# Loading the last 96 rows of a weight matrix as 68 + 28 rows, in two transfers with a semaphore each

## The chip, the cores and the metric

The kernel runs on one core of a Trainium2 chip. The metric is the device time of one execution in microseconds (us). A ratio compares the fast runs of two kernels of the same rounds and stands here, with its 95% interval, as the record has it; it is not quite the ratio of the medians or means that are quoted. Where "means" are given, it is the difference between the mean of a kernel's runs and that of the runs of before beside it.

Of the engines, PE multiplies matrices (PEld is the weight load that comes before each product), DVE computes on vectors, and SP issues the loads here.

## The reference, cut to what matters

One token of two sequences goes through a decode step: layer norm, attention of 32 heads over 8192 cached positions, a residual, layer norm, a gated feed-forward block (D = 512, F = 1376), a residual.

```python
h  = x + attention(layernorm(x), k_cache, v_cache, wq, wo)   # caches: 2 x 32 x 8192 x 128, bf16
g  = layernorm(h) @ W_gate                                   # 512 x 1376
u  = layernorm(h) @ W_up
h2 = h + (max(g, 0) * u) @ W_down                            # 1376 x 512
```

The caches are 256 MiB and are read once. W_down has 1376 rows: ten blocks of 128 and a rest of 96. The change is about that rest.

## The kernel before

K and V of a pair of heads come as one transfer each, into four slots. At the end slot 0 is free and takes W_up, W_gate and the first 1280 rows of W_down; the last 96 rows have a buffer of their own, `wd_last`, with one row in each partition. SP issues all of these in a row, 25 to 28 us before they are first used:

```python
WD_BLOCKS = ((0, 4), (4, 4), (8, 2))
# ... (cut)
wd_last = sb("wd_last", [FR, D], BF16)                       # FR = 96, D = 512: 1 KB a row
# ... (cut) SP, when slot 0 is free:
for k, w in enumerate((B_W_up, B_W_gate)):
    nc.sync.dma_start(slot[0][...], w...).then_inc(sem_w[k], 16)
for k, (r0, n) in enumerate(WD_BLOCKS):
    nc.sync.dma_start(slot[0][...], B_W_down[r0 * 128:(r0 + n) * 128]...).then_inc(sem_wd[k], 16)
nc.sync.dma_start(wd_last[:], B_W_down[F - FR:]).then_inc(sem_wd[3], 16)
```

At the very end PE runs the down projection in the order in which the blocks arrive, with a wait in front of each, then DVE scales and adds the residual, and the result is stored:

```python
order = [(f, k) for k, (r0, n) in enumerate(WD_BLOCKS) for f in range(r0, r0 + n)] + [(10, 3)]
for n, (f, k) in enumerate(order):
    pe.wait((sem_wd[k], 16))
    kp = 128 if f < 10 else FR
    for m in range(4):
        i = nc.tensor.matmul(Op[0][32 * m:32 * m + B, 0:128], lhsT=hd[0:kp, f * B:(f + 1) * B],
                             rhs=(wdn[:, f, :] if f < 10 else wd_last[:])[:, 128 * m:128 * m + 128],
                             start=(n == 0), stop=(n == FC - 1))
```

I call the three WD_BLOCKS transfers block 1, 2 and 3.

The softmax here doesn't subtract the row's maximum and nothing guards it: scores larger than these inputs give would overflow.

## Time and profile before

| | before |
|---|---|
| median, first 3 runs | 660.2 us (660.03 to 660.39) |
| span of the profiled run | 659.2 us |
| HBM traffic | 281 MB at a mean 427 GB/s |
| SP issues the load of wd_last | 628.22 us |
| its 16 landings | 654.13 to 656.06 us |
| PE's first weight load that reads wd_last | 656.28 us |

The page's DMA lines, before. The first row is the busy share of the 16 DMA engines in 40 slices of the span, in tenths:

```profile
DMA  8999999999999999999999999999999999999997
GB/s 366 444 437 431 420 445 416 443 428 431 438 422 441 422 439 433 428 435 424 441 422 439 433 428 433 426 441 422 439 434 426 435 424 441 424 437 433 428 417 295
DMA packets 10653, 281.17 MB, mean 427 GB/s; under 512 B 1202, under 2 KB 1300, under 8 KB 1812
```

The stream never pauses until the last slice. Dividing 281 MB by 427 GB/s gives 658 us, so nearly the whole span is the stream. Only what happens while it runs out can be changed by this edit. The table of windows, before (columns: window, its length, busy time and instruction count of PE, PEld, DVE, ACT and POOL, then granted PE clock, DMA share, GB/s):

```profile
641.00:648.00 7.00, 6.99 (x71) 2.30 (x68) 1.63 (x4) 1.55 (x8) 0.00 (x0) 0.58 0.99 413
...
652.00:653.00 1.00, 1.00 (x35) 0.98 (x36) 0.04 (x1) 0.00 (x0) 0.00 (x0) 0.50 1.02 397
...
654.00:655.00 1.00, 1.00 (x35) 0.98 (x33) 0.00 (x0) 0.00 (x0) 0.00 (x0) 0.50 0.43 157
...
655.50:656.00 0.50, 0.50 (x28) 0.50 (x24) 0.07 (x1) 0.00 (x0) 0.00 (x0) 0.50 0.16 33
656.00:656.50 0.50, 0.50 (x28) 0.41 (x16) 0.00 (x0) 0.00 (x0) 0.00 (x0) 0.50 0.00 0
```

The DMA share falls from 1.02 to 0.16 over three microseconds: the 16 engines run dry one after another. The chain that ended last, in order of time, before (start, duration, what):

```profile
655.13 0.19 DVE hd L789
...
655.36 1.37 PE O L808 x23
...
656.85 0.35 DVE kT L815
```

The end is a chain of compute: the gated product hd, the down projection, the residual. The timeline, before: the issues of W_up and of wd_last on SP, and the weight loads of the down projection.

```profile
625.95 0.33 SPq L699 DMA_DIRECT2D slot<-in_B_W_up_dram  x1
...
628.22 2.39 SPq L706 DMA_DIRECT2D wd_last<-in_B_W_down_dram  x1
...
655.36 0.95 PEld L808 LDWEIGHTS O<-slot,hd 128*2 128x2 bf16 x40 [0.32 <-DVE hd L789]
...
656.28 0.13 PEld L808 LDWEIGHTS O<-wd_last,hd 96*2 96x2 bf16 x4
```

There is no gap in front of the wd_last weight loads: the data came 0.22 us before the first of them. The trace also records each increment that a DMA makes on its semaphore; I call them landings. Here are the latest of them, before, in us (not a view of the profile, but read from the trace):

```
block 3: 16 landings, 653.90 ... 655.57 655.69 655.71 655.86
wd_last: 16 landings, 654.13 ... 655.84 655.91 655.92 656.06
```

### The profile page before, as it was taken

What the parts mean: (1) busy time and instruction counts of PE and PEld (TensorE: products, weight loads), DVE (VectorE), ACT (ScalarE), POOL (GpSimd) and SP (SyncE); (2) the same over time, 40 slices, a digit from 0 to 9 for tenths busy, and PEclk for the clock granted to TensorE, in tenths of its full rate; (3) what the DMA queues carried; (4) which work ended last, traced back from release to release, by engine and by line L of the source; (5) the groups of instructions that cost most, each with busy time, mean ns of one, the idle gap of its engine ahead of it and who ended that gap; (6) DMA issues with size and microseconds to landing.
All of it is one profiled execution on the core that took longest, in us unless ns stands there. A gap on an engine that the chain in (4) does not pass through costs nothing.

```text
span 659.2 us, 7582 instructions
## 1 busy us (share of the span) xinstructions
PE 324.3 (49%) x3073; PEld 188.6 (29%) x3073; DVE 469.2 (71%) x280; ACT 213.6 (32%) x431; POOL 73.5 (11%) x125
## 2 busy tenths in 40 slices
PE   2753454435455343655535364443556444354577
PEld 0331332213233121433313142221324222133344
DVE  1585576788767678776768877676886767787991
ACT  1622333143342223334223343422324332333250
POOL 3002002020200202020020201002020110202000
PEclk9856556565756657555665756756555765655656
DMA  8999999999999999999999999999999999999997
GB/s 366 444 437 431 420 445 416 443 428 431 438 422 441 422 439 433 428 435 424 441 422 439 433 428 433 426 441 422 439 434 426 435 424 441 424 437 433 428 417 295
DMA packets 10653, 281.17 MB, mean 427 GB/s; under 512 B 1202, under 2 KB 1300, under 8 KB 1812
## 3 DMA queue, kind: packets, MB, share of 16 engines
q1 hardware_dynamic: 10632, 281.06, 99.3%
q8 instruction: 5, 0.08, 0.1%
q14 instruction: 4, 0.03, 0.0%
q10 hardware_dynamic: 12, 0.00, 0.0%
HBM read 281.05 MB, written 0.00 MB: 426 GB/s over the span
## 4 chain that ended last, share of the span: by engine, by line
DMA 76%; DVE 19%; PE 4%; issue 1%; ACT 1%; SPq 0%; DVEq 0%
DMA slot<-in_A_k_cache_dram 76%; DVE prod L540 16%; DVE prod L549 2%; PE O L405 1%; PE O L463 1%; PE T L381 0%; ACT kT L566 0%; PE W L469 0%; DVE scores L554 0%; PE S L756 0%; PE O L756 0%; PE O L808 0%; PE Ob L417 0%; SPq L172 0%; PE S L364 0%
## 5 line engine op out<-in xcount | busy, mean ns | idle before, releaser
L540 DVE TENSOR_TENSOR prod<-slot,q_c 128x12288 bf16<-128x12288 bf16 x32 | 209.9, 6558 | 148.0 <-DMA slot<-in_A_k_cache_dram 141.3
L405 PE MATMUL O<-slot,e 128*16 128x512 bf16 x1024 | 119.3, 621 | 219.9 <-ACT e L495 146.2
L549 DVE TENSOR_TENSOR prod<-prod 128x6144 bf16<-128x6144 bf16 (+3 forms) x128 | 212.2, 1657 | 7.8
L566 ACT ACTIVATE kT<-T 128x1024 bf16<-128x1024 bf16 x128 | 126.1, 1022 | 144.6 <-PE T L381 141.9
L381 PE MATMUL T<-ident_f,slot 128*128 128x128 f32 x512 | 108.6, 365 | 29.1 <-DVEq L587 29.1
L405 PEld LDWEIGHTS O<-slot,e 128*16 128x16 bf16 x1024 | 26.4, 114 | 287.0 <-ACT e L495 172.9
L495 ACT ACTIVATE e<-scores 64x96 bf16<-64x96 f32 x64 | 19.5, 304 | 239.6 <-DVEq L601 238.9
L381 PEld LDWEIGHTS T<-ident_f,slot 128*128 128x128 f32 x512 | 79.0, 188 | 44.2 <-DVEq L587 43.3
L537 POOL COPY q_c<-q_all 128x136 bf16<-128x136 bf16 x32 | 57.2, 1788 | 195.5 <-DVEq L591 152.5
L364 PE MATMUL S<-q_c,kT 128*128 128x4 bf16 x1024 | 47.4, 168 | 40.8 <-ACT kT L566 40.0
L364 PEld LDWEIGHTS S<-q_c,kT 128*128 128x128 bf16 x1024 | 39.1, 104 | 67.9 <-ACT kT L566 66.8
L417 PE MATMUL Ob<-sel,os_sb 128*128 128x4 f32 x136 | 30.1, 345 | 24.2 <-ACT os_sb L569 24.2
L417 PEld LDWEIGHTS Ob<-sel,os_sb 128*128 128x128 f32 x136 | 28.6, 311 | 26.1 <-ACT os_sb L569 26.1
L520 POOL MEMSET O_l<- 128x40 bf16 (+1 forms) x13 | 1.8, 136 | 303.9 <-DVEq L598 303.9
L554 DVE TENSOR_REDUCE scores<-prod 128x96 f32<-128x768 bf16 x32 | 30.5, 953 | 2.8
L566 ACT ACT_TABLE_LOAD x15 | 19.2, 1283 | 0.3
L495 ACT ACTIVATE e<-S 64x32 bf16<-64x32 f32 x64 | 13.0, 202 | 15.1 <-PE S L364 14.7
L569 ACT ACTIVATE os_sb<-O 128x512 f32<-128x512 f32 x17 | 10.1, 597 | 12.8 <-PE O L405 12.4
L495 ACT ACTIVATION_READ_ACCUMULATOR e<-S 64x1 f32 x64 | 12.8, 201 | 0.7
L495 ACT ACTIVATION_READ_ACCUMULATOR e<-scores 64x1 f32 x64 | 11.8, 185 | 0.0
L426 PEld LDWEIGHTS Ob<-zs,ones_f 128*128 128x128 f32 x30 | 7.1, 296 | 12.5 <-issue 12.5
L525 POOL COPY rsel<-rows 128x30 bf16<-128x30 bf16 x28 | 5.9, 209 | 33.3 <-DVEq L598 32.5
(104 smaller groups left out, 90.6 us busy)
## 6 DMA issues: line engine op xcount, KB each, us to landing
slot<-in_A_k_cache_dram SPq DMA_DIRECT2D x32, 4096.0 KB, 32.1
slot<-in_A_v_cache_dram SPq DMA_DIRECT2D x31, 4096.0 KB, 30.3
slot<-in_A_wq_dram SPq DMA_DIRECT2D x1, 4096.0 KB, 12.2
X<-in_A_wo_dram SPq DMA_DIRECT2D x1, 3840.0 KB, 45.8
slot<-in_A_v_cache_dram SPq DMA_DIRECT2D x1, 3072.0 KB, 23.3
slot<-in_B_W_up_dram SPq DMA_DIRECT2D x1, 1376.0 KB, 23.2
slot<-in_B_W_gate_dram SPq DMA_DIRECT2D x1, 1376.0 KB, 26.2
slot<-in_A_v_cache_dram SPq DMA_DIRECT2D x1, 1024.0 KB, 25.4
```

The lines of the kernel that those rows point to most:

```text
L364: i = nc.tensor.matmul(Sp[p % 2][:, 2 * jj:2 * jj + 4], lhsT=kv_[:, k, r, :], rhs=q_c[p % 2][:, 4 * r:4 * r + 4], start=(r == 0), stop=(r ...
L381: i = nc.tensor.transpose(Tp[g % 2][:, k * 128:(k + 1) * 128], k_t[:, j:j + 2, :].rearrange("p j d -> p (j d)").bitcast(F32), ident_f[:])
L405: i = nc.tensor.matmul(Op[0][c:c + 16, :], lhsT=e_t[q][:, j // VJ, :], rhs=v_t[:, j:j + VJ, :].rearrange("p j d -> p (j d)"), start=(q == ...
L417: i = nc.tensor.matmul(Ob[:, 0:4], lhsT=os_sb[:, jj * Dh:(jj + 1) * Dh], rhs=sel[:, 4 * jj:4 * jj + 4], start=(jj == 0), stop=(jj == VJ - 1))
L426: return nc.tensor.matmul(bank[:, ZC:ZC + 8], lhsT=ones_f[:], rhs=zs[:], start=True, stop=True)
L495: i = nc.scalar.activation(out=e_t[q][h, j0 // VJ:j1 // VJ, 8 * q:8 * q + 8].rearrange("p g (j a) -> p g j a", a=2)[:, :, :, a], in_=src(h ...
L537: nc.gpsimd.tensor_copy(out=q_c[p % 2][:], in_=q_all[:, p]).then_inc(g2d, 1)
L540: return nc.vector.tensor_tensor(out=prod[:, 0:JC, :], in0=tile((2 * p) % 4)[:, 0:JC, :], in1=q_c[p % 2][:, 8:QW].unsqueeze(1).broadcast_t ...
L549: run(nc.vector.tensor_tensor(out=prod[:, 0:JC, 0:w], in0=prod[:, 0:JC, 0:w], in1=prod[:, 0:JC, w:2 * w], op=ALU.add))
L554: return nc.vector.tensor_reduce(out=scores[p % PG][:, 0:JC], in_=prod[:, 0:JC, 0:8], axis=AX.X, op=ALU.add)
L566: to_pe(nc.scalar.activation(out=kT[gg % 2][:], in_=Tp[gg % 2][:].bitcast(BF16), func=ACT.Copy))
L569: to_pe(nc.scalar.activation(out=os_sb[:], in_=Op[0][:], func=ACT.Copy))
```

## The change

The intent is to bring the rest in as two pieces, each with its own semaphore. PE waits for both before the one matmul that reads them, so nothing starts earlier by design.

```diff
+    WD_TAIL = ((0, 68), (68, 28))
...
-        sem_wd = [S(f"wd{i}") for i in range(4)]
+        sem_wd = [S(f"wd{i}") for i in range(5)]
...
-                        nc.sync.dma_start(wd_last[:], B_W_down[F - FR:]).then_inc(sem_wd[3], 16)
+                        for k, (r0, n) in enumerate(WD_TAIL):
+                            nc.sync.dma_start(
+                                wd_last[r0:r0 + n], B_W_down[F - FR + r0:F - FR + r0 + n]).then_inc(sem_wd[3 + k], 16)
...
-                    pe.wait((sem_wd[k], 16))
+                    pe.wait((sem_wd[k], 16), (sem_wd[max(k, 2 * k - 2)], 16))
```

## The prediction

> **What bounds the kernel now.** The stream from HBM. The page shows the 16 DMA engines at 9 tenths in nearly every slice, and 281 MB at a mean 427 GB/s: 658 of the 659.2 us span; the chain that ended last is 76% DMA of the K cache. Only the end is not covered: the table of windows has the DMA share falling from 1.02 (652 to 653 us) to 0.43 (654 to 655), 0.16 (655.5 to 656) and 0. From 641 us the chain, in order of time, is compute: last P·V, normalisation, up, gate, the down projection (1.37 us from 655.36), one DVE instruction (0.35 us), and the store, to 659.2.
>
> **How close wd_last is to that chain.** SP issues it at 628.22 us and it lands 27.8 us later, queued behind other loads. The landing records of its semaphore show 16 increments, one for each DMA engine, from 654.13 to 656.06 us. PE reaches the first weight load of wd_last at 656.28 us without a gap. So the slack is 0.22 us; whatever makes the last engine later by more is on the critical path.
>
> **What the change does.** Same bytes, same 1 KB packets. The Trainium skill, "DMA: Bandwidth & Descriptors", section "Why a DMA increments its semaphore by 16 and not by 1", says that a transfer uses the largest number of engines, up to 16, that divides its slowest dimension. The trace agrees where it can: 96 rows gave 16 landings, each 4-row store 4 completion packets. So 68 rows should go over 4 engines (17 packets each) and 28 rows over 14 (2 each). Four engines carry 19 packets instead of 6, ten carry 2, two none. A 1 KB packet takes 46 ns in the trace, so the four finish about 13 x 46 = 0.6 us later (estimate), the others about 0.2 us earlier.
>
> Whether it costs depends on where those four stand in the 1.9 us spread, which the trace doesn't tell. If one is among the five latest (655.67 to 656.06), the 68 rows land at 656.3 to 656.7, and PE waits 0 to 0.4 us before wd_last. If all are early, nothing happens. I put 65% on some wait.
>
> Other costs: a second issue on SP (96 rows took 2.39 us to issue, 128 rows 0.33 to 0.43), done by about 633 us, when SP has nothing else until 657.2. A second semaphore wait on PE, some tens of ns, on the chain. Nothing that helps is removed: the matmul waits for both parts.
>
> **Predicted.** 660.2 + about 0.2 = 660.4 us, range 659.5 to 661.3 (the runs of before alone spread 0.36 us). Faster by over 2%: 0.5%; within 2%: 99%; slower by over 2%: 0.5%.
>
> **What would show it.** Two wd_last issues, the first with 4 data landings, the second with 14; as many 1 KB packets as before; the 68-row part landing last, 0.3 to 0.7 us later than 656.06 relative to the stream's end; a new gap of PE before wd_last, released by DMA, of up to 0.4 us, and the store later by as much. All before 650 us unchanged. If the four engines are early: both landings before 656.1 and no gap.
>
> **What would make it wrong.** The 68 rows going to one engine only: 68 x 46 ns = 3.1 us, so up to 3 us later. Or a 17-row share far slower than 46 ns a packet. Or the slow SP issue blocking something I don't see. None reaches 2%.

## The result, and the profile after

The median of 6 runs is 660.33 us (660.24 to 660.74), beside 660.17 us (660.03 to 660.39, 6 runs) before. The ratio is 1.0003, with a 95% interval of 0.999 to 1.0016: the same. All outputs are right.

The page, after: the packets. Two more than before, both of the small completion kind.

```profile
DMA packets 10655, 281.17 MB, mean 427 GB/s; under 512 B 1204, under 2 KB 1302, under 8 KB 1814
```

Before, this load had 16 completion packets; 4 + 14 = 18 is two more. The landings in the trace, after:

```
block 3:  16 landings,                      653.86 ... 655.71 655.93 656.09
68 rows:   1 record at 629.81, then  4:     655.00 655.42 655.47 655.86
28 rows:   1 record at 641.06, then 14:     654.10 ... 655.88 656.05 656.14
```

So the 68 rows went over 4 engines and the 28 rows over 14, and the one early record of each comes 0.12 and 0.18 us after SP's issue ended. This agrees with the Trainium skill, "DMA: Bandwidth & Descriptors", section "Why a DMA increments its semaphore by 16 and not by 1", which says that the engines used are the largest divisor up to 16 of the slowest dimension, and that the issuing sequencer adds the missing count at once. But the four engines with 17 packets did not end last. The timeline, after:

```profile
625.45 0.33 SPq L700 DMA_DIRECT2D slot<-in_B_W_up_dram  x1
...
627.74 13.14 SPq L708 DMA_DIRECT2D wd_last<-in_B_W_down_dram  x2
...
654.98 0.31 PEld L811 LDWEIGHTS O<-slot,hd 128*2 128x2 bf16 x16 [0.32 <-DVE hd L792]
...
655.54 0.31 PEld L811 LDWEIGHTS O<-slot,hd 128*2 128x2 bf16 x16 [0.26 <-DMA slot<-in_B_W_down_dram]
656.13 0.10 PEld L811 LDWEIGHTS O<-slot,hd 128*2 128x2 bf16 x8 [0.28 <-DMA slot<-in_B_W_down_dram]
656.24 0.12 PEld L811 LDWEIGHTS O<-wd_last,hd 96*2 96x2 bf16 x4
```

Two things are new. SP spends 13.14 us on the two issues; one line of the tile view of wd_last, after, splits them (minimum/median/maximum, ns):

```profile
L708 SPq DMA_DIRECT2D wd_last<-in_B_W_down_dram x2: 1944/6548/11152, 627.7 to 629.7; - x2
```

And PE now waits for DMA, but in front of blocks 2 and 3, whose loads the change doesn't touch, and not in front of wd_last. The chain that ended last, after, goes through a DMA that is not wd_last either.

```profile
625.82 27.04 DMA slot<-in_B_W_gate_dram
...
652.91 1.73 PE O L759 x44
...
654.75 0.19 DVE hd L792
...
654.98 1.68 PE O L811 x35
...
656.76 0.35 DVE kT L818
```

Compute was ahead of the stream in this profile (the down projection starts at 654.98, against 655.36), and behind it in the profile before. The table of windows, after, shows what went with that: PE was granted a clock of 0.81 in the window of the last P·V products (attention weights times V), against 0.58 before.

```profile
641.00:648.00 7.00, 5.69 (x69) 2.25 (x70) 1.94 (x5) 2.16 (x9) 0.00 (x0) 0.81 1.00 419
```

Nothing in the change touches that stage. The two profiles also differ before it: SP came to the first load for slot 0, that of W_up, at 625.95 us before and at 625.45 us after, and to wd_last only after that, so this much of the difference was there before an edited instruction ran. Over all profiles the issue of W_up lies between 625.18 and 627.92 us. Two single profiles therefore can't say what the change costs, and the experiments begin by repeating both kernels.

### The profile page after: what moved, and what is told of

The parts are those of the page before. It is cut to its first block, busy times and chain, and to the rows that moved or that the text cites. A ratio compares the mean times of both kernels' runs of the same rounds, so it can differ in the third digit from the quotient of the medians.

```text
span 659.0 us, 7584 instructions
## 1 busy us (share of the span) xinstructions
PE 322.5 (49%) x3073; PEld 187.6 (28%) x3073; DVE 469.3 (71%) x280; ACT 213.7 (32%) x431; POOL 73.6 (11%) x125
## 4 chain that ended last, share of the span: by engine, by line
DMA 80%; DVE 18%; issue 1%; PE 1%; SPq 0%; DVEq 0%
DMA slot<-in_A_k_cache_dram 76%; DVE prod L541 16%; DMA slot<-in_B_W_gate_dram 4%; DVE prod L550 2%; PE O L759 0%; PE O L811 0%; DVE scores L555 0%; SPq L173 0%; DVEq L588 0%; DVEq L592 0%; SPq L176 0%; SPq L177 0%; DVE kT L818 0%; DVE hd L792 0%; DVEq L604 0%
## 5 line engine op out<-in xcount | busy, mean ns | idle before, releaser
L406 PE MATMUL O<-slot,e 128*16 128x512 bf16 x1024 | 117.6, 613 | 220.4 <-ACT e L496 146.5
```

Source lines behind the costliest of these rows:

```text
L406: i = nc.tensor.matmul(Op[0][c:c + 16, :], lhsT=e_t[q][:, j // VJ, :], rhs=v_t[:, j:j + VJ, :].rearrange("p j d -> p (j d)"), start=(q == ...
```

## The experiments

Twelve runs of kernels followed, in three groups of four; x1 to x9 and y1 to y5 are their numbers in the table below. The kernels of one group share their 9 runs of before on the same chip. The groups ran on different chips, with medians of before of 660.54, 660.36 and 660.49 us, so an expectation that gives a time is to be read against these. Theory A is that the share of the busiest engine decides, together with where that engine stands in the order in which the engines run dry. The rivals are that the split itself costs something (a second transfer, a second wait), and that wd_last doesn't matter to the time at all.

### Both kernels again

No edit.

> The kernel before, unchanged, to see how far one profile differs from the next. All theories: 660.2 us within 0.2. The landings of wd_last end within about 0.4 us of 656.06 us; PE waits at most 0.2 us in front of wd_last. If the latest landing moves by 0.3 us or more from profile to profile, the 0.16 us between the medians of before and after can't be assigned from two profiles.

> The changed kernel, unchanged. Theory A (share of the engines): 68 rows go over engines that stand early or in the middle of the spread, so their 17 packets are absorbed: the 68-row part lands before the 28-row part, no PE gap before wd_last, time 660.2 to 660.5 us. Rival B (the split itself costs: second wait on PE, second transfer): 0.1 to 0.2 us over the kernel before in every round. The issue of the 28 rows takes about 11 us on SP again.

Measured: before 660.54 us (5 runs) beside 660.54; after 660.71 us beside 660.54, ratio 1.0001. The means differ by -0.07 and by +0.05 us. The second issue on SP took 11.28 us again. The landings of after repeat: the 68 rows end at 655.84, block 3 at 656.16, the 28 rows at 656.33. PE's first wd_last weight load came at 656.43, 0.105 us after the 28 rows; from the step of the loads in front of it (0.107 us for four) it would have come at 656.30, so PE did wait about 0.13 us (estimate), for the 28 rows, where I had expected no gap.

The records of the trace also show what the second wait costs (not a view of the profile; x2, the changed kernel, in us):

```
block 3: last landing 656.155; first weight load, which carries the wait itself, 656.197
28 rows: last landing 656.329; wait instruction (EVENT_SEMAPHORE) 656.358, 0.051 long;
         first weight load of wd_last, which carries the wait for the 68 rows, 656.434
```

A load that carries its only wait starts 0.042 us after the landing; with the extra wait instruction in front of it, 0.105 us. In the kernel before, the load of wd_last carries its only wait and there is no such instruction. So where PE stands at this wait, the second semaphore adds about 0.06 us to the chain.

### The same split with the packets spread as before: 64 + 32

```diff
-    WD_TAIL = ((0, 68), (68, 28))
+    WD_TAIL = ((0, 64), (64, 32))
```

> Two transfers and two waits as in the change, but 64 and 32 rows, which both spread over 16 engines (4 + 2 packets each, as many as before). Theory A: as before, 660.2 us within 0.15, 16 landings each, last landing about 0.25 us after the last of the third W_down block. Rival B: as the change, 660.3 to 660.4. SP issues of 0.33 to 0.45 us each if only counts that are no power of two are slow to issue, else 2 us and more.

Measured: 660.66 us beside 660.54, ratio 1.0000; means +0.08 us. Each part has 16 landings. The last comes 0.33 us after the last of block 3, against 0.20 us of x1: a second transfer on the same engines lands later, even with the same packets in all (0.33 us again in y3, and 0.20 to 0.25 us in the three profiles of before). The SP issues took 0.61 and 1.15 us, which neither branch of my guess about powers of two foresaw. The split costs nothing that this can resolve.

### One engine takes nearly everything: 89 + 7

```diff
-    WD_TAIL = ((0, 68), (68, 28))
+    WD_TAIL = ((0, 89), (89, 7))
```

> Two transfers, but 89 rows, a prime, so that one engine should carry 89 packets, and 7 rows over seven engines. Theory A (the share of the busiest engine decides, at 43 to 46 ns a packet): that engine lands 3.9 to 4.1 us after its part of the third block (654.2 to 655.1 us), so at 658.1 to 659.2; PE waits 1.8 to 3.0 us before wd_last; 662.2 to 663.3 us. Rival C (wd_last is not near the critical path, or the split costs the same at every size): 660.3 us.

Measured: 662.18 us beside 660.54, ratio 1.0025 (1.0011 to 1.0038), means +1.64 us. The 89 rows have a single data landing, at 657.77; the last of the 7-row part comes at 657.95. The timeline of 89 + 7:

```profile
655.66 0.94 PEld L811 LDWEIGHTS O<-slot,hd 128*2 128x2 bf16 x40 [0.32 <-DVE hd L792]
...
658.06 0.12 PEld L811 LDWEIGHTS O<-wd_last,hd 96*2 96x2 bf16 x4 [1.45 <-DMA wd_last<-in_B_W_down_dram]
```

The new wait of 1.45 us in front of wd_last is most of the 1.64 us by which the kernel got slower. Rival C falls: wd_last can hold up the end. The time, the landing and the wait are all under the ranges that I gave, probably because the one engine was among the first to run dry: 89 packets of 43 ns, the spacing of back-to-back packets in the trace, before 657.77 is 653.9, where block 3 had its first landings (653.93). The SP issue of the 7 rows took 21.01 us.

### The parts in the other order: 28 + 68

```diff
-    WD_TAIL = ((0, 68), (68, 28))
+    WD_TAIL = ((0, 28), (28, 68))
```

> The same two parts in the other order: 28 rows first, 68 rows second; the rows of a part differ, not its size. Theory A on the time: the engines' shares are the same, so as the change, 660.3 to 660.7 us beside 660.5 of before; the 68-row part again lands before 656.1 us. On the SP issue, theory Q (the issue of a transfer waits until the one before it fits into the queues of its engines): 28 rows issue in under 2.5 us, and so do the 68 rows, as nothing stands behind them; SP is done by about 633 us. Rival I (28 rows over 14 engines are slow to issue by themselves): 11 us for the 28 rows, now the first.

Measured: 660.3 us beside 660.36, ratio 0.9999. The landings are those of the change (68 rows end at 656.04, 28 rows at 656.13). The timeline of 28 + 68, SP:

```profile
630.01 1.30 SPq L708 DMA_DIRECT2D wd_last<-in_B_W_down_dram  x2
```

The two issues took 0.46 and 0.79 us. So 28 rows are not slow to issue by themselves, rival I falls, and theory Q stands: it is what lies in front that holds up an issue. The runs make a series of it. The issue of the second part took, by the packets that the first part put on each of its engines: 0.79 us after 2 packets (28 + 68), 1.15 us after 4 (64 + 32), 6.39 us after 7 (91 + 5), 11.15 us after 17 (the change), 17.99 us after 43 (86 + 10) and 21.01 us after 89 (89 + 7). The issue of the first part (or of the whole wd_last) varies too: 1.9 to 2.9 us in the six profiles in which SP came to it at 627.5 to 628.2 us, and 0.33 to 0.87 us in the seven in which it came at 629.9 to 630.3 us. That full queues are the reason is inferred from this and from the early load below; no record of the profile shows a queue's fill, and the second parts differ in rows and engines as well.

### 91 + 5

```diff
-    WD_TAIL = ((0, 68), (68, 28))
+    WD_TAIL = ((0, 91), (91, 5))
```

> 91 rows over seven engines (13 packets each) and 5 rows over five (1 each): the engines that landed last in the third block get nothing. Theory A: both parts have landed by 655.9 us, before the third block's last landing (about 656.05); PE never waits for wd_last itself; 660.2 to 660.6 us beside 660.5 of before, so at most 0.2 us gained, since the kernel before has next to no wait there to win back. Rival (the slow engines' 6 packets cost the kernel before something): 0.2 to 0.3 us less in every round.

My expectation was wrong about the engines: 13 also divides 91 and is the larger, and the trace has 13 data landings, not 7. Each had 7 packets. Measured: 660.45 us beside 660.36, ratio 1.0001. Both parts had landed by 655.93, before the last landing of block 3 at 656.17, as expected; and nothing was gained (means +0.15 us). In this profile PE came to wd_last at 656.85 without a wait.

### A middle dose: 86 + 10

```diff
-    WD_TAIL = ((0, 68), (68, 28))
+    WD_TAIL = ((0, 86), (86, 10))
```

> A middle dose: 86 rows over two engines (43 packets each), 10 rows over ten (1 each), so 44 packets on the busiest engine against 6, 19 and 90. Theory A: 44 x 44 ns = 1.9 us after those engines' part of the third block (653.95 to 655.1 us), so they land at 655.9 to 657.0; PE waits 0 to 0.6 us; 660.4 to 661.1 us. A straight line through 6 and 90 packets would give +0.75 us, 661.3; a threshold gives 0.1 to 0.5.

Measured: 660.94 us beside 660.36, ratio 1.0009 (0.9996 to 1.0023), means +0.52 us. The two engines landed at 656.10 and 656.31, the 10-row part at 656.49. The timeline of 86 + 10:

```profile
656.59 0.12 PEld L811 LDWEIGHTS O<-wd_last,hd 96*2 96x2 bf16 x4 [0.23 <-DMA wd_last<-in_B_W_down_dram]
```

This lies just above the branch with a threshold (0.1 to 0.5) and below the straight line (0.75), so it doesn't tell the two apart; the profile, with a wait of 0.23 us, was taken of the fastest of the five runs. Three of the five runs are slower than every run of before in the group, which points to a cost of 44 packets on the busiest engine that 19 don't have; but the interval of the ratio contains 1, so the cost isn't shown clear of noise.

### The parts at the start

```diff
+                for k, (r0, n) in enumerate(WD_TAIL):
+                    nc.sync.dma_start(
+                        wd_last[r0:r0 + n], B_W_down[F - FR + r0:F - FR + r0 + n]).then_inc(sem_wd[3 + k], 16)
                 load(0, A_k_cache, 0)
...
-                        for k, (r0, n) in enumerate(WD_TAIL):
-                            nc.sync.dma_start(
... (cut)
```

> 68 and 28 rows as in the change, but loaded at the start, behind wq and the last rows of wo, into the same buffer, which nothing else uses. Theory A: the end of the stream is then the third W_down block; PE has no wait for wd_last; the total bytes are the same, so the stream ends about as late as before less nothing: 660.2 to 660.7 us. Theory Q on the issue: no backlog stands in front, so both issues take under 1 us; rival I: 28 rows take about 11 us here too.

Measured: 660.63 us beside 660.36, ratio 1.0006 (0.9993 to 1.002), means +0.35 us: no gain, and perhaps a loss (the interval contains 1). In the one profile block 3 landed last, at 656.33, against 655.86 to 656.06 in the three profiles of before. The bytes that now come earlier in the stream could account for 0.23 us of that (an estimate: 96 KiB at 427 GB/s); the rest is not explained. On the issue, theory Q holds again. The timeline of the early load, SP:

```profile
1.72 0.91 SPq L180 DMA_DIRECT2D wd_last<-in_B_W_down_dram  x2
```

With only the loads of wq and of the last rows of wo in front, 68 and 28 rows issue in 0.91 us together, against 13.14 us at the end. The 28 rows stand behind the same 17 packets on each of four engines here and took 0.49 us, so the part in front alone doesn't hold up an issue; it points to all that is still queued.

### Is there a cost of 0.1 to 0.2 us after all?

The first comparison had +0.22 us between the means, the second +0.05. So four kernels ran again, with no new edit.

> The kernel before once more, as the control of this group: within 0.1 us of the runs of before in the same rounds. It gives a third profile of it: PE's first weight load of wd_last comes 0.1 us after the last landing or later, without a wait of over 0.2 us.

> The changed kernel once more. Is the 0.1 to 0.2 us between the means of before and after real? If the change costs (28 rows on 14 engines that include a late one, 0.17 us behind the third block; or the second wait): mean 0.1 to 0.25 us above before in these rounds too. If it was chance: within 0.1 us. SP's second issue again about 11 us.

> 28 rows, then 68 rows, once more: the same packets on the same engines, without the long issue on SP. If a cost of the change came from the long issue, this one is within 0.1 us of before and the change is not; if from the packets' places, both are alike.

> 64 and 32 rows once more: the second transfer and the second wait with the packets spread as before. If these two cost 0.1 us or more, the mean lies that much above before; if not, within 0.1 us. Last landing about 0.3 us after the third block's last, in each profile.

Measured, against 9 runs of before with a mean of 660.49 us: before +0.00, after -0.03, 28 + 68 -0.14, 64 + 32 +0.06 us. For the changed kernel the three comparisons are +0.22, +0.05 and -0.03 us, and one kernel's runs within a group spread by 0.2 to 0.8 us. The cost is not resolved: it is chance, or under about 0.2 us. The 0.06 us of the second wait, which the traces show, is too small for these runs.

y5, the repeat of 28 + 68, shows that the race can go the other way. Its profile had early compute, and PE did wait for the 68-row part, whose last landing was at 656.12. The timeline of y5:

```profile
655.86 0.10 PEld L811 LDWEIGHTS O<-slot,hd 128*2 128x2 bf16 x8 [0.37 <-DMA slot<-in_B_W_down_dram]
656.22 0.12 PEld L811 LDWEIGHTS O<-wd_last,hd 96*2 96x2 bf16 x4 [0.26 <-DMA wd_last<-in_B_W_down_dram]
```

Still this span, 658.9 us, is the shortest of all profiles. So a short wait for wd_last doesn't by itself show that time was lost; it can come of early compute.

All profiles with wd_last at the end, in us. "Down projection" is its first weight load; "last landing" is the later of the two parts; "first use" is the first weight load that reads wd_last.

| profile | down projection | block 3 last landing | wd_last last landing | first use | first use minus landing | span |
|---|---|---|---|---|---|---|
| before | 655.36 | 655.86 | 656.06 | 656.28 | 0.22 | 659.2 |
| x1 before | 655.49 | 656.06 | 656.26 | 656.41 | 0.15 | 659.3 |
| y1 before | 655.78 | 656.04 | 656.29 | 656.69 | 0.41 | 659.6 |
| after (68 + 28) | 654.98 | 656.09 | 656.14 | 656.24 | 0.10 | 659.0 |
| x2 after | 655.15 | 656.16 | 656.33 | 656.43 | 0.10 | 659.1 |
| y2 after | 654.87 | 656.17 | 656.37 | 656.48 | 0.10 | 659.2 |
| x5 28 + 68 | 655.56 | 655.93 | 656.13 | 656.47 | 0.34 | 659.3 |
| y5 28 + 68 | 654.76 | 655.82 | 656.12 | 656.22 | 0.10 | 658.9 |
| x3 64 + 32 | 655.66 | 656.04 | 656.37 | 656.58 | 0.20 | 659.5 |
| y3 64 + 32 | 654.97 | 656.21 | 656.54 | 656.65 | 0.10 | 659.4 |
| x6 91 + 5 | 655.94 | 656.17 | 655.93 | 656.85 | 0.93 | 659.7 |
| x9 86 + 10 | 655.41 | 656.04 | 656.49 | 656.59 | 0.10 | 659.4 |
| x4 89 + 7 | 655.66 | 655.86 | 657.95 | 658.06 | 0.10 | 660.8 |

The column before the last has a floor of 0.10 us, which includes the extra wait instruction of the kernels with two parts. In front of blocks 2 and 3, where the load carries its only wait, the same step is 0.04 us in all 12 waits of six profiles (after, x2, y2, y3, y5 and the early load). A profile that stands on the floor either waited for wd_last or, as after, met it with nothing to spare. The others were held by compute. 64 + 32 and 28 + 68 were seen on both sides, so the side isn't a property of a kernel with two parts. The three profiles of before are all held by compute and the three of after all by the stream; whether before would be seen on the other side too, no profile shows. How early compute is goes along with a time before wd_last is issued: W_up was issued at 625.2 to 625.8 us in the five profiles whose down projection began before 655.2, and at 625.95 us or later in all the others.

## Why the prediction was right or wrong

The time was right: 660.4 predicted, 660.33 measured, within 2%. The edit leaves the bytes alone, the stream sets the span, and 19 packets on four engines still fit into the spread in which the engines run dry (89 + 7 has the same bytes and costs 1.64 us). That the two numbers agree to 0.1 us is luck: the predicted 0.2 us were for a wait for the 68 rows that did not come, and the measured difference is not resolved.

- **The engines: right.** 4 and 14 data landings, and as many 1 KB packets as before (98 in each trace, two of them of the load of x).
- **"The 68-row part landing last, 0.3 to 0.7 us later than 656.06": wrong.** It ended at 655.86, 655.84 and 655.90 in the three profiles of after, and the 28-row part last, at 656.14, 656.33 and 656.37. I had put 65% on some wait, which needed one of the four engines to stand among the five latest. They did not stand there: 17 packets at 43 ns before 655.86 is about 655.1 (estimate), where 11 of the 16 landings of block 3 had come, so most of the extra 13 packets a head went into time in which those engines would have been idle. The branch that came true is close to "if the four engines are early", in the first profile; "both landings before 656.1" was already missed there by 0.04 us, and in the other two by more, because of the 28 rows.
- **"The slack is 0.22 us": mis-sized.** From a landing to the load that waits for it there are 0.04 us even where PE stands at the wait and the load carries it, as it does in before. So the slack in the profile before was about 0.17 us (estimate; no profile of before waits for wd_last). With the second wait instruction of the change, 0.10 of the 0.22 us are needed (seven of the table's profiles, 89 + 7 among them). One profile was also too little to read it from: the first use moves between 656.22 and 656.85 in kernels whose wd_last was not made late on purpose.
- **"A new gap of PE before wd_last, up to 0.4 us": not in the first profile.** The second and third, worked out the same way, have about 0.13 and 0.16 us (estimates), for the 28 rows and not the 68. Such waits came with early compute: the spans of these two profiles (659.1 and 659.2 us) are not longer than those of before (659.2 to 659.6 us).
- **"All before 650 us unchanged": wrong.** The last P·V products ended at 647.99 us before and at 646.96 us after, with granted clocks of 0.58 and 0.81 from 641 to 648 us. As the issue of W_up shows, profiles already differ at 625 to 628 us. That the clock is the cause of early compute is argued from these windows, not shown by an experiment.
- **"Second issue on SP, done by about 633 us": wrong.** It was done at 640.9. I took 2.39 us for the price of 96 rows; x1 paid 0.56 us for the same instruction. An issue here costs what the backlog in front of it makes it cost: 11.15 us behind 68 rows and 21.01 us behind 89 rows at the end of the stream, and 0.91 us for both parts together at its start. It was harmless because SP had nothing else to do until 657.
- **"A second wait on PE, some tens of ns": right where PE waits.** It is an instruction of its own of 0.051 us, and the load starts 0.10 instead of 0.04 us after the landing. In the time it isn't resolved: 64 + 32 has both waits, and landings that come 0.1 us later, and is +0.08 and +0.06 us.

## What to carry to other kernels

A transfer's row count chooses how many DMA engines carry it, and each engine's packets, added to where that engine stands when the stream runs dry, decide when the transfer lands; 90 packets on one engine cost 1.64 us here and 44 on two engines perhaps half a microsecond, while 19 hid in the spread. When two chains end within 0.2 us of each other, take several profiles of each kernel before you assign a wait to an edit: here the wait moved from compute to DMA and back with no edit at all. And if the issuing engine has other work to do, put the transfer with the most packets for each of its engines last when much is queued already: behind 17 packets an engine, an issue of 28 rows took 11 us there, and under 1 us at the start of the kernel.

## What the Trainium skill lacked or had wrong

- "DMA: Bandwidth & Descriptors", section "Why a DMA increments its semaphore by 16 and not by 1": the rule for the number of engines held for every count tried (96, 64 and 32 rows: 16; 68: 4; 28: 14; 89: 1; 7: 7; 91: 13; 5: 5; 86: 2; 10: 10). Nothing to mend.
- "DMA: Bandwidth & Descriptors", section "Issuing engines are not separate DMA queues", calls the sequencer's time to initiate a DMA "usually small relative to the DMA itself". It lacks that, behind a backlog, an issue is held up the longer, the more packets the transfer in front put on each engine: from 0.79 us behind 2 packets to 11.15 us behind 17 and 21.01 us behind 89, against 0.91 us for two issues together (68 and 28 rows) at the start of the kernel.
- The same page, section "Rules for kernel authors", says of two transfers to disjoint partition halves that they are not worth it. 64 + 32, though not halves, fits: +0.08 and +0.06 us in the means, no gain.
- The same page, section "Latency and other measured facts", names engines 7 and 15 as usually slower and ties that to descriptors made by GpSimd, as its best guess. This kernel has no such transfers, and its engines still end 2.2 us apart (block 3 of after: 653.86 to 656.09). In 89 + 7 the 7-row part, which by the page's rule goes to the seven lowest-numbered engines, has three landings from 655.70 to 655.95, among the late ones, so late engines are not 7 and 15 alone.
- No page that I read gives the time from a landing to the PE weight load that waits for it, or what a second wait adds: 0.04 us where the load carries its only wait (12 cases in six profiles), and 0.10 us with one more wait instruction in front of it (seven profiles).
